# Attention with sketched keys, then a SiLU layer: V arrives as bf16 through GpSimd's queue, and the task list is new

## The chip, the cores and the metric

The kernel runs on one core of a Trainium2 chip. The metric is the device time of one execution in microseconds (us), and lower is better. The core has a matrix engine (TensorE, PE in the profile, with its weight loads as PEld), VectorE (DVE), ScalarE (ACT), GpSimd (POOL) and SyncE (SP), which here only issues transfers. Each engine works through its own instructions in order and waits for the others at semaphores.

## The reference: what is computed

There are four batches and four heads, 1088 tokens and 32 numbers per head. Two small matrices S1 and S2 (8 by 32) make 64 features of each query and key; attention is then linear in these features, and its output goes through a layer of 2048 hidden units.

```python
def phi(x):
    a = np.einsum('rd,bhsd->bhsr', S1, x)
    b = np.einsum('rd,bhsd->bhsr', S2, x)
    return np.einsum('bhsi,bhsj->bhsij', a, b).reshape(*x.shape[:-1], r * r)
q_p, k_p = (phi(q), phi(k))
kv = np.einsum('bhsf,bhsd->bhfd', k_p, v)
z = np.sum(k_p, axis=2)
num = np.einsum('bhsf,bhfd->bhsd', q_p, kv)
den = np.einsum('bhsf,bhf->bhs', q_p, z)[..., None] + 1e-06
# x: (num / den), its heads side by side: 4352 tokens x 128
h = x @ w_in                        # 128 x 2048
g = h * (1.0 / (1.0 + np.exp(-h)))
out = g @ w_out                     # 2048 x 128
```

## The kernel before

Every step of the work is a named task. A batch's function adds tasks under names such as `KV2.3`, and the string `ORDER` lists all names; the tasks are recorded in that order, so each engine gets its instructions in that order too. No scheduler moves anything later. The first number in a name is the batch, or the block of the layer for H, A, O and F.

For each batch b the tasks are these.
- `LK`, `LQ`, `LV` load keys, queries and values. Batch 0's keys and queries come in two parts, and V of every batch in four transfers of 32 partitions each (`load_v`). All of them are issued by SP.
- `KT` transposes keys on DVE, `PK` projects them on PE, `TK` transposes the result back on DVE.
- `KP` forms the 64 products of each key. It is two large DVE instructions for batch 0 and nine small POOL instructions for batches 1 to 3 (`KN`); after each of these POOL also runs a memset of one element, `pause`.
- `VB` casts V from fp32 (`Vx`, two tiles that the batches take in turn) to bf16 (`Vb`). It is on ACT for batches 0 and 1 and on POOL for 2 and 3.
- `KV` sums products times V on PE, `KM` masks the sum, `SE` spreads it over partitions on PE, and `KC` copies it to `KV[b]`.
- `ZS`, `ZT`, `MW`, `WM` make the weights of the denominator in the same way. They go into `WQ[b]`, the weights of the query projection. `WR` copies the fixed part of `WQ` to the other batches, on POOL.
- Queries come in pieces, three for batch 0 and two for each other batch. A piece runs `QT` (transpose, DVE), `PQ` (projection, PE), `TQ` (transpose, DVE), `AW`, `RD`, `RC`, `AQ`, `QP` (denominator and products, DVE), `TN` (transpose, DVE), `NM` (numerators, PE) and `XC` (copy to `xT`, on ACT for batches 0 and 1, on DVE for 2 and 3).

`PK`, `PQ` and `NM` all write the one PSUM tile `pair`, so each of them waits until its reader before has emptied it.

The layer runs over ten blocks of tokens, of 384, seven times 512, 256 and 128. `H` multiplies by two columns of `w_in` (PE), `A` is the SiLU (ACT), `O` multiplies by `w_out` (PE), and `F` moves the block's result out of PSUM (DVE) and stores it through SP. H writes two PSUM tiles by turns (three from block 7 on), so ACT and PE hand buffers to each other. Block 1 needs all pieces of batch 0; block 2 needs the first piece of batch 1; block 4 the first of batch 2, block 5 its second; block 6 the first of batch 3.

`LI` and `LO` load the fp32 weights of the layer; `wi.0` to `wi.3` cast quarters of `w_in` on ACT, and `wo.0` to `wo.3` quarters of `w_out` on POOL. O0.0 and O0.1 need `wo.0`, O0.2 and O0.3 need `wo.1`, and so on. The tasks `f.0` to `f.106` are matmuls of zeros (128 columns) that fill PE's time before the layer starts; each stands at a fixed place of the list.

At the start, the list in the kernel before has on PE: `PQ0.0`, 8 fills, `KV0.0 KV0.5`, 9 fills, `SE0`, 23 fills, `NM0.0`, 10 fills, `PQ0.2`, one fill, `H0.0 H0.1`.

Of the kernel before, what the change touches and what calls it, by code (L numbers as in the profile page):

```python
# [57 lines left out]
H3 = 7  # L58
ORDER = """
S2 LK0.0 LK0.1 begin KT0.0 KT0.1 LQ0.0 QT0.0 LV0.0 LV0.1 LV0.2 LV0.3 begin2 S1 f.0 f.1 f.2 f.3 f.4 f.5 f.6  # L60
f.7 f.8 f.9 SM SN table WQ0 WK L4 f.10 f.11 f.12 f.13 f.14 f.15 f.16 f.17 f.18 f.19 f.20 f.21 f.22 f.23 f.24
PK0.0 PK0.1 TK0.0 TK0.1 f.25 f.26 f.27 f.28 f.29 f.30 f.31 f.32 f.33 ZS0 ZT0 f.34 f.35 f.36 f.37 f.38 f.39
f.40 f.41 MW0 WM0 f.42 f.43 f.44 f.45 f.46 f.47 f.48 f.49 f.50 PQ0.0 KP0.0 KP0.5 TQ0.0 AW0.0 RD0.0 RC0.0
AQ0.0 QP0.0 TN0.0 VB0 f.51 f.52 f.53 f.54 f.55 f.56 f.57 f.58 KV0.0 KV0.5 KM0 f.59 f.60 f.61 f.62 f.63 f.64
f.65 f.66 f.67 SE0 KC0 f.68 f.69 f.70 f.71 f.72 f.73 f.74 f.75 f.76 f.77 f.78 f.79 f.80 f.81 f.82 f.83 f.84
f.85 f.86 f.87 f.88 f.89 f.90 NM0.0 LI.0 wi.0 wi.2 wi.3 XC0.0 wi.1 LQ0.1 LO.0 LO.1 wo.1 wo.0 wo.2 wo.3 WR
LK1 LV1.0 LV1.1 LV1.2 LV1.3 QT0.1 QT0.2 f.91 f.92 f.93 f.94 f.95 f.96 f.97 f.98 f.99 f.100 PQ0.2 TQ0.2 AW0.2
RD0.2 RC0.2 f.101 H0.0 H0.1 A0.0 f.102 PQ0.1 f.103 f.104 f.105 f.106 H0.2 O0.0 A0.1 TQ0.1 AW0.1 AQ0.2 RD0.1
QP0.2 RC0.1 TN0.2 AQ0.1 KT1 QP0.1 LQ1 LK2 LV2.0 LV2.1 LV2.2 LV2.3 LQ2 LK3 H0.3 A0.2 O0.1 H0.4 A0.3 A0.4 O0.2
H0.5 A0.5 NM0.2 O0.3 H0.6 XC0.2 H0.7 A0.6 A0.7 PK1 O0.4 O0.5 O0.6 TK1.1 TK1.0 TN0.1 KP1.0 KP1.1 KP1.2 KP1.3  # L70
KP1.4 KP1.5 KP1.6 KP1.7 KP1.8 ZS1 VB1 ZT1 NM0.1 O0.7 MW1 KV1.0 WM1 QT1.0 LV3.0 LV3.1 LV3.2 LV3.3 LQ3 XC0.1
H1.0 A1.0 H1.1 KV1.1 KV1.2 PQ1.0 KV1.3 KV1.4 H1.2 F0 QT1.1 O1.0 A1.1 KV1.5 H1.3 A1.2 A1.3 TQ1.0 AW1.0 RD1.0
KT2 RC1.0 KV1.6 O1.1 H1.4 O1.2 KV1.7 KV1.8 H1.5 PK2 A1.4 KM1 A1.5 H1.6 SE1 O1.3 O1.4 O1.5 H1.7 AQ1.0 QP1.0
TK2.0 TK2.1 TN1.0 A1.6 KC1 NM1.0 XC1.0 A1.7 O1.6 ZS2 PQ1.1 H2.0 ZT2 A2.0 O1.7 H2.1 KT3 TQ1.1 AW1.1 F1 MW2
PK3 WM2 RD1.1 RC1.1 TK3.1 AQ1.1 QP1.1 TK3.0 TN1.1 QT2.0 QT3.0 A2.1 H2.2 A2.2 KP2.0 KP2.1 KP2.2 KP2.3 KP2.4
KP2.5 VB2 KP2.6 KP2.7 VB3 KP2.8 KP3.0 KP3.1 KP3.2 KP3.3 KP3.4 KP3.5 KP3.6 KP3.7 KP3.8 H2.3 O2.0 A2.3 KV2.0
KV2.1 KV2.2 KV2.3 KV2.4 KV2.5 O2.1 H2.4 O2.2 A2.4 H2.5 O2.3 KV2.6 KV2.7 NM1.1 H2.6 A2.5 H2.7 KV2.8 O2.4
XC1.1 A2.6 ZS3 PQ2.0 ZT3 A2.7 KM2 H3.0 O2.5 O2.6 O2.7 SE2 H3.1 TQ2.0 AW2.0 QT2.1 RD2.0 RC2.0 F2 A3.0 A3.1
H3.2 KC2 PQ2.1 MW3 A3.2 KV3.0 H3.3 A3.3 KV3.1 O3.0 H3.4 KV3.2 O3.1 H3.5 O3.2 A3.4 A3.5 TQ2.1 AQ2.0 QP2.0
TN2.0 H3.6 A3.6 NM2.0 XC2.0 AW2.1 RD2.1 RC2.1 AQ2.1 QP2.1 TN2.1 KV3.3 H3.7 A3.7 O3.3 KV3.4 H4.0 O3.4 KV3.5  # L80
H4.1 O3.5 A4.0 KV3.6 H4.2 A4.1 O3.6 H4.3 O3.7 KV3.7 A4.2 H4.4 A4.3 NM2.1 KV3.8 H4.5 F3 WM3 XC2.1 O4.0 A4.4
A4.5 H4.6 PQ3.0 H4.7 O4.1 A4.6 H5.0 QT3.1 TQ3.0 PQ3.1 AW3.0 TQ3.1 KM3 RD3.0 AW3.1 RC3.0 A4.7 H5.1 A5.0 O4.2
H5.2 O4.3 SE3 KC3 AQ3.0 QP3.0 TN3.0 RD3.1 A5.1 H5.3 A5.2 O4.4 H5.4 O4.5 O4.6 A5.3 H5.5 A5.4 O4.7 H5.6 NM3.0
O5.0 A5.5 H5.7 XC3.0 RC3.1 A5.6 A5.7 O5.1 H6.0 O5.2 O5.3 H6.1 A6.0 O5.4 H6.2 A6.1 A6.2 AQ3.1 QP3.1 TN3.1 F4
NM3.1 O6.0 XC3.1 H6.3 O5.5 A6.3 H6.4 A6.4 O5.6 H7.0 A7.0 H6.5 O6.1 H6.6 O6.2 O6.3 O5.7 A6.5 H6.7 H7.3 A6.6
F5 A6.7 H7.1 A7.1 A7.3 O6.4 O6.5 H7.2 O6.6 O7.0 H7.4 O6.7 H7.6 A7.2 H7.5 O7.1 A7.4 A7.6 H7.7 O7.2 O7.3 O7.4
A7.5 F6 A7.7 H8.0 A8.0 H8.1 O7.5 H8.2 O7.6 A8.1 A8.2 H8.3 A8.3 O7.7 H9.0 O8.0 O8.1 H9.1 O8.2 O8.3 H9.2 A9.0
F7 A9.1 A9.2 O9.0 O9.1 O9.2 F8 F9
# [4 lines left out]
def kernel(  # L93
# [19 lines left out]
    CH = 512  # L113
# [14 lines left out]
    Vx = [sb(f"Vx{i}", [H * NC * D]) for i in range(2)]  # L128
# [422 lines left out]
    for b in range(B):  # L551
        batch(b, KN[b], PIECES[b], XENG[b], KVENG[b])
# [34 lines left out]
```

## Time and profile before

| what | value |
|---|---|
| median of three runs | 94.6 us (94.59, 94.6, 96.18) |
| the profiled execution | 95.22 us, of which the span is 93.4 us |
| granted TensorE clock | 1.0 |
| PE busy | 87.5 us (94%) |
| ACT busy | 76.3 us (82%) |
| DVE busy | 59.3 us (63%) |
| POOL busy | 26.4 us (28%) |
| read from HBM, written | 8.79 MB, 2.23 MB |

The span is the time between the first and last recorded instruction; 1.82 us of the profiled execution lie around it. Times in the profile are counted from the span's start. A waiting matmul that is already in the pipeline counts as busy, so a busy PE is not a PE at its best rate. Issues of transfers are not counted as busy time of the engine that issues them.

### The profile page before, as it was taken

The numbers are of one execution on the slowest core, as the hardware profiler recorded it, in microseconds if no ns is written. First come the engines' busy times: TensorE is split into PE (matmuls) and PEld (weight loads), VectorE is DVE, ScalarE is ACT, GpSimd is POOL, SyncE is SP. The second block draws the span as 40 slices with busy tenths as digits, with TensorE's granted clock in tenths as the row PEclk, the third lists the DMA queues.
The fourth block names the chain that finished last, engine by engine and source line by source line (L and its number), as shares of the span: only waits on it lengthen the run. The fifth ranks groups of instructions, "written<-read, shape, count | busy, mean of one in ns | idle before, by whom it ended". The sixth has DMA issues, their size and how long they took to land.

```text
span 93.4 us, 2184 instructions
## 1 busy us (share of the span) xinstructions
PE 87.5 (94%) x813; PEld 46.7 (50%) x823; DVE 59.3 (63%) x114; ACT 76.3 (82%) x102; POOL 26.4 (28%) x91
## 2 busy tenths in 40 slices
PE   5999989999999999999999999999999999999950
PEld 4948776544543443544444443344344444456940
DVE  2369796999499969983986978489597030300330
ACT  4800687999599868899699999999898999999930
POOL 6700008300993299999900000000000000000000
PEclk9999999999999999999999999999999999999999
DMA  0999999999968730600024003300001404133151
GB/s 19 334 256 343 374 408 318 245 291 238 309 202 222 229 77 14 112 0 7 0 39 73 0 0 63 56 0 0 0 0 29 70 14 85 34 56 60 31 115 50
DMA packets 21898, 11.15 MB, mean 119 GB/s; under 512 B 17152, under 2 KB 20608, under 8 KB 21760
## 3 DMA queue, kind: packets, MB, share of 16 engines
q1 hardware_dynamic: 21704, 10.95, 44.7%
q8 instruction: 6, 0.10, 0.4%
q10 hardware_dynamic: 184, 0.07, 0.3%
q14 instruction: 4, 0.03, 0.1%
HBM read 8.79 MB, written 2.23 MB: 118 GB/s over the span
## 4 chain that ended last, share of the span: by engine, by line
PE 83%; DVE 9%; issue 2%; POOL 2%; DVEq 0%; POOLq 0%
PE hp L181 28%; PE op L181 27%; PE pair L181 14%; PE small L181 14%; DVE QP L192 2%; DVE TQ L435 2%; DVE QU L455 2%; DVE AW L192 1%; DVE TK L368 1%; DVE DN L442 1%; DVE DN L445 1%; DVE AQ L192 0%; POOL hmask L245 0%; POOL Vx L251 0%; DVE OT L540 0%
## 5 line engine op out<-in xcount | busy, mean ns | idle before, releaser
L519 ACT ACTIVATE G<-hp 128x1024 bf16<-128x1024 f32 (+1 forms) x66 | 60.9, 989 | 4.6 <-PE hp L181 2.9
L181 PE MATMUL hp<-xT,w_in_bf 128*128 128x512 bf16 (+3 forms) x137 | 36.2, 355 | 0.2
L181 PE MATMUL op<-G,w_out_bf 128*128 128x512 bf16 (+1 forms) x93 | 25.8, 370 | 0.2
L181 PEld LDWEIGHTS <-w_in_bf 128*128 128x128 bf16 x160 | 13.7, 98 | 13.3 <-issue 2.8
L192 POOL TENSOR_TENSOR KP<-TK 128x256 bf16<-128x256 f32 x27 | 17.0, 631 | 9.2 <-DVE TK L368 9.2
L181 PEld LDWEIGHTS <-w_out_bf 128*128 128x128 bf16 x128 | 11.6, 98 | 12.5 <-issue 1.1
L181 PE MATMUL op<-zeros 128*128 128x128 bf16 x107 | 10.1, 255 | 1.0 <-DVE zeros L240 1.0
L192 DVE TENSOR_TENSOR QP<-AQ,TQ 128x1024 bf16<-128x1024 f32 (+3 forms) x9 | 10.8, 1195 | 0.2
L181 PEld LDWEIGHTS <-zeros 128*128 128x128 bf16 x107 | 7.9, 116 | 3.0 <-issue 1.7
L181 PE MATMUL small<-G,w_out_bf 128*128 128x512 bf16 x31 | 8.8, 379 | 0.1
L435 DVE STREAM_TRANSPOSE TQ<-pair 128x512 f32<-128x512 f32 (+3 forms) x9 | 6.1, 675 | 3.7 <-PE pair L181 2.8
L546 DVE STREAM_TRANSPOSE OT<-small 128x512 f32<-128x512 f32 x2 | 1.4, 716 | 9.3 <-PE small L181 9.3
L355 DVE STREAM_TRANSPOSE KT<-Kx 128x1152 f32<-128x1152 f32 (+1 forms) x5 | 5.6, 1135 | 2.2 <-DMA Kx<-in_k_dram 2.1
L546 DVE STREAM_TRANSPOSE OT<-op 128x512 f32<-128x512 f32 (+1 forms) x6 | 4.0, 667 | 4.1 <-PE op L181 4.1
L181 PEld LDWEIGHTS <-KP 128*128 128x128 bf16 x72 | 4.3, 98 | 4.0 <-issue 0.4
L455 DVE STREAM_TRANSPOSE QU<-QP 128x512 f32<-128x512 f32 (+3 forms) x9 | 6.0, 665 | 0.2
L424 DVE STREAM_TRANSPOSE QT<-Qx 128x512 f32<-128x512 f32 (+3 forms) x9 | 5.7, 653 | 0.3 <-DMA Qx<-in_q_dram 0.3
L181 PE MATMUL pair<-QT,WQ 64*64 64x256 f32 (+3 forms) x72 | 5.7, 389 | 0.1
L181 PE MATMUL small<-Vb,KP 128*128 128x64 bf16 x72 | 5.3, 193 | 0.1
L519 ACT ACTIVATE G<-pair 128x1024 bf16<-128x1024 f32 x5 | 5.2, 1037 | 0.0
L189 POOL CAST w_out_bf<-w_out_f 128x512 bf16<-128x512 f32 x4 | 2.3, 612 | 9.9 <-DMA w_out_f<-in_moe_w_out_dram 9.9
L187 DVE CAST xT<-pair 128x512 bf16<-128x512 f32 (+4 forms) x6 | 3.4, 615 | 2.2 <-PE pair L181 2.2
(68 smaller groups left out, 73.0 us busy)
## 6 DMA issues: line engine op xcount, KB each, us to landing
Vx<-in_v_dram SPq DMA_DIRECT2D x12, 144.0 KB, 9.1
Kx<-in_k_dram SPq DMA_DIRECT2D x3, 544.0 KB, 12.3
Qx<-in_q_dram SPq DMA_DIRECT2D x3, 544.0 KB, 8.8
w_in_f<-in_moe_w_in_dram SPq DMA_DIRECT2D x1, 1024.0 KB
w_out_f<-in_moe_w_out_dram SPq DMA_DIRECT2D x2, 512.0 KB, 9.2
out_dram<-OT SPq DMA_DIRECT2D x16, 64.0 KB, 1.9
Vx<-in_v_dram SPq DMA_DIRECT2D x4, 112.0 KB, 7.2
Qx<-in_q_dram SPq DMA_DIRECT2D x1, 352.0 KB, 7.8
```

What stands on the lines that cost most here:

```text
L181: nc.tensor.matmul(dst, w, x, start=start, stop=stop, tile_position=pos, **kw)
L187: nc.vector.tensor_copy(out=out_, in_=in_)
L189: nc.gpsimd.tensor_copy(out=out_, in_=in_)
L192: (nc.vector if eng == "D" else nc.gpsimd).tensor_tensor(out=out_, in0=a, in1=c, op=ALU.mult)
L355: o.add(f"KT{b}{at}", lambda c0=c0, c1=c1: nc.vector.transpose(out=view(kt[:, :], c0 * 32, (32, c1 - c0), (P, NC), (1, 32)), in_=Kx[b][:, ...
L368: o.add(f"TK{b}.{r}", lambda r=r: nc.vector.transpose(out=view(tk[:, :], 16 * r, (32, NC), (NC * 32, 2), (1, 16)), in_=view(pair[:, :], r ...
L424: o.add(f"QT{b}.{p}", lambda n0=n0, n1=n1: nc.vector.transpose(out=qt[:, n0 * 64: n1 * 64], in_=Qx[b][:, n0 * 64: n1 * 64]))
L435: o.add(f"TQ{b}.{p}", lambda at=at, m=m: nc.vector.transpose(out=tq[:, at * 32: (at + 2 * m) * 32], in_=view(pair[:, :], 0, (CH, 2), (1, m ...
L442: o.add(f"RD{b}.{p}", lambda at=at, rn=rn: nc.vector.tensor_reduce(out=dn[:, at: at + rn], in_=view(aw[:, :], at * 9, (9, rn), (1, 9)), ax ...
L455: o.add(f"TN{b}.{p}", lambda at=at, rn=rn: nc.vector.transpose(out=qu[:, at * 64: (at + rn) * 64].bitcast(FP32), in_=qp[:, at * 64: (at + ...
L519: nc.scalar.activation(out=view(gb[:, :], 0, (stride, per), (1, ntok)), in_=view(hb[:, :], 0, (stride, per), (1, ntok)), func=ACT.Silu)
L546: nc.vector.transpose(out=t[:, :ntok], in_=ob[:, :ntok])
```

## The change

V of every batch is now loaded by GpSimd's queue, straight into the bf16 tiles, so that the transfer itself makes bf16 of fp32. The tiles `Vx` and the four `VB` tasks are gone. The products of batch 3's keys are two DVE instructions (`KP3.0`, `KP3.5`) in place of nine on POOL. `HOLDS` makes the first transfer of V of batch 1 wait for the first half of `w_out`. The list is new. The diff below leaves out functions whose new forms issue the same instructions as before: `project_q`, `tokens_q`, `numerators` and `back` can now also cut a piece of more than 16 units and put parts on other engines, and with the tables given they do neither.

```diff
-KN = [[('D', 0, 5), ('D', 5, 9)], [('P', 0, 1), ... ('P', 8, 9)], [('P', 0, 1), ...], [('P', 0, 1), ...]]
+KN = [[('D', 0, 5), ('D', 5, 9)], [('P', 0, 1), ... ('P', 8, 9)], [('P', 0, 1), ...], [('D', 0, 5), ('D', 5, 9)]]
-VB_ENG = 'AAPP'
-HOLDS = {}
+HOLDS = {'LV1.0': 'LO.0'}
...
-    Vx = [sb(f"Vx{i}", [H * NC * D]) for i in range(2)]
...
     def load_v(b, c):
         n = min(NC, NY - c * NC)
-        return nc.sync.dma_start(
-            view(Vx[b % 2][32 * c: 32 * (c + 1), :], 0, (NC * D, H), (1, n * D)),
+        return nc.gpsimd.dma_start(
+            view(Vb[b][32 * c: 32 * (c + 1), :], 0, (NC * D, H), (1, n * D)),
             AP(tensor=v.tensor, offset=v[b, 0, c * NC].offset,
                ap=[[NY * D, 32], [S * D, H], [1, n * D]]))
...
     def begin2():
-        nc.gpsimd.memset(view(Vx[1][96:P, :], (NY - 3 * NC) * D, (NC * D, H),
-                              (1, (4 * NC - NY) * D)), 0.0)
         nc.gpsimd.memset(view(AW[1][:, :], 8, (9, 2 * NN)), 1e-6)
         for b in range(1, B):
             nc.gpsimd.memset(view(WQ[b][:, :], 16, (32, 2), (1, 16)), 0.0)
             nc.gpsimd.memset(view(Kx[b][:, :], NY * D, (1, (4 * NC - NY) * D)), 0.0)
+            nc.gpsimd.memset(view(Vb[b][96:P, :], (NY - 3 * NC) * D, (NC * D, H),
+                                  (1, (4 * NC - NY) * D)), 0.0)
...
-    for b in range(B):
-        o.add(f"VB{b}", lambda b=b: copy(VB_ENG[b], Vb[b], Vx[b % 2]))
```

The new list, cut to the stretches that the prediction speaks of:

```
S2 LK0.0 LK0.1 begin KT0.0 S1 table f.0 ... f.9 SM WK SN L4 KT0.1 WQ0 LV0.0
begin2 LV0.1 LV0.2 LV0.3 LQ0.0 LI.0 LQ0.1 LO.0 LO.1 LK1 LQ1 LK2 LQ2 LK3 LQ3 wo.0 LV1.0 LV1.1 LV1.2 LV1.3
wo.2 wo.1 WR LV2.0 wo.3 QT0.0 f.10 ... f.24
PK0.0 PK0.1 TK0.0 TK0.1 KP0.5 KP0.0 f.25 ... f.33 ZS0 ZT0 f.34 ... f.41 MW0 WM0 f.42 ... f.50
PQ0.0 TQ0.0 AW0.0 RD0.0 RC0.0 AQ0.0 QP0.0.0 TN0.0.0 f.51 ... f.72
KV0.0 wi.2 wi.1 KV0.5 KM0 wi.0 f.73 ... f.81 SE0 KC0 f.82 ... f.90 NM0.0 XC0.0.0 wi.3 QT0.2 QT0.1 f.91 ...
f.100 PQ0.2 TQ0.2 AW0.2 RD0.2 RC0.2 f.101 H0.0 H0.1 A0.0 f.102 PQ0.1 A0.1 f.103 ... f.106
H0.2 A0.2 O0.0 O0.1 H0.3 O0.2 H0.4 A0.3 TQ0.1 AQ0.2 AW0.1 KT1 RD0.1 QP0.2.0 RC0.1 A0.4 PK1 H0.5 A0.5 TK1.1
AQ0.1 TN0.2.0 TK1.0 KP1.0 ... KP1.8 QP0.1.0 TN0.1.0 O0.3 H0.6 O0.4
H0.7 A0.6 ZS1 NM0.2 O0.5 O0.6 A0.7 XC0.2.0 ZT1 NM0.1 MW1 KV1.0 KV1.1 O0.7 XC0.1.0 H1.1 A1.1 KT2 PK2 QT1.0
...
O1.6 O1.7 XC1.0.0 H2.0 A2.0 LV2.1 LV2.2 LV2.3 LV3.0 LV3.1
KP2.0 KP2.1 KP2.2 LV3.2 LV3.3 KP2.3 ... KP2.8 H2.1
...
PQ2.0 A2.4 H2.6 KV2.2 KV2.3 KV2.4 KV2.5 O2.3 TQ2.0 KP3.0 QT2.1 AW2.0 RD2.0 RC2.0 AQ2.0 QP2.0.0 TN2.0.0 A2.5
...
O3.2 A3.7 QT3.1 XC2.0.0 WM3 H4.0 A4.0 PQ3.0 KP3.5 AQ2.1 QP2.1.0 TQ3.0 TN2.1.0 H4.1 A4.1 KV3.0 H4.2 O3.3 O3.4
...
H5.5 NM3.0 A5.4 A5.5 H5.6 O4.7 O5.0 A5.6 H5.7 XC3.0.0
TN3.1.0 NM3.1 XC3.1.0 F4 H6.0 O5.1
```

## The prediction

> **What bounds the kernel now.** I read the busy shares first, then the chain that ended last, in order of time, then the timelines of ACT and POOL and the landing times of V. Busy times and shares:
>
> ```profile
> PE 87.5 (94%) x813; PEld 46.7 (50%) x823; DVE 59.3 (63%) x114; ACT 76.3 (82%) x102; POOL 26.4 (28%) x91
> PE 83%; DVE 9%; issue 2%; POOL 2%; DVEq 0%; POOLq 0%
> ```
>
> PE bounds most of the span, and POOL, where the change works, carries 2% of the chain. The 9% of DVE lie early, as the chain in order of time shows (start, length, what):
>
> ```profile
> 13.43 0.59 DVE QU L455
> 14.02 0.04 issue
> 14.06 0.36 PE pair L181 x7
> ...
> 19.36 0.42 DVE QU L455
> 19.78 0.04 issue
> 19.82 0.34 PE pair L181 x8
> ...
> 23.08 0.47 DVE QU L455
> 23.55 0.04 issue
> 23.59 0.36 PE pair L181 x7
> ```
>
> The reader sees each piece of batch 0 end with its transpose on DVE (`TN0`), for which PE's numerators wait: at 14.02, 19.78 and 23.55. Block 1 starts at 24.6. From there on PE hardly stops. A pair of 512-column matmuls takes 0.432 in the chain; blocks 1 to 9 are 124 of them, 53.6 us, and what is left of attention is about 10.3 (PK 2 x 0.65, PQ 3.75, NM 2.3, KV 1.6, ZS, MW and SE 1.4). That is 63.9 of the 65.5 us up to the last matmul at 90.1. So after 24.6 only 1.6 us can be won, and between 15.5 and 24.6 about 1 us, if no DVE link of the early chain becomes shorter.
>
> **The early chain, DVE part.** The new list leaves the order of DVE's work up to `TN0.0` as it was, with the same durations, and the same number of fills ahead of `PQ0.0`. So `TN0.0` ends at 14.0 again, and that is the earliest time of `NM0.0`. Nothing is won here.
>
> **VB0 goes from ACT, and V comes otherwise.** This is what ACT did before (start, length, what):
>
> ```profile
> 9.74 1.16 ACT L185 ACTIVATE Vb<-Vx 128x1152 bf16<-128x1152 f32 x1
> 11.73 0.52 ACT L279 ACTIVATE KM<-small,pmask 128x64 bf16<-128x64 f32 x2 [0.83 <-PE small L181]
> 12.61 0.38 ACT L185 ACTIVATE KV<-small 128x256 bf16<-128x256 f32 x1 [0.36 <-PE small L181]
> ```
>
> V was used from 10.95 on, and KV0 was ready at 12.99, one us before `NM0.0` could use it. The new list spends this us: 22 fills (0.061 each in this stretch: 0.67 for 10, in the chain) stand ahead of `KV0.0` instead of 8, so its turn comes at 10.55 + 1.38 = 11.93; sums 0.55, mask 0.55 with its wait, then `wi.0` 0.62 stands ahead of `KC0` 0.38: 14.03. The cast's 1.16 on ACT is therefore worth nothing, and each tenth that V is later than 12.0 is a tenth later for everything, because DVE's chain for the other two pieces starts from `XC0.0`.
>
> When does V land? The trace has no transfer issued by POOL. The first comes behind the memsets of `begin`, at 3.1; the rest behind `begin2`, which takes 1.4 now and about 2.1 with two more memsets (0.31 each). For the issue itself the bounds are SP's issue row (0.31 at least, 0.43 in this stretch) and a whole cast of V on POOL (1.19 undisturbed). I take 0.63, the row of POOL's small product, as a POOL instruction over 128 partitions. Then the last issue ends at 3.1 + 2.1 + 4 x 0.63 = 7.7. From issue to landing:
>
> ```profile
> Vx<-in_v_dram SPq DMA_DIRECT2D x3, 144.0 KB, 3.9
> ...
> Vx<-in_v_dram SPq DMA_DIRECT2D x3, 144.0 KB, 10.1
> ```
>
> The first row holds the issues before 6 us, the second those between 6 and 14: V of batch 1, far back in a full queue. A queue of its own does not stand behind SP's, but the 16 DMA engines are shared and fully busy from 3 to 25 us in both lists. I take the longest of the first three, 4.4: V lands at 12.1, loss 0.15 to 0.2. Bounds: 3.8 after issues of 0.31 gives 10.3, no loss; issues of 1.19 and 4.4 give 14.4, loss 2.3; a landing of 8.6, the median of all V transfers, gives 16.3, loss 4.3.
>
> The Trainium skill, page "DMA: Bandwidth & Descriptors", section "Anatomy of one DMA — SWDGE (gpsimd) path", gives a transfer of this queue as 2.0 us plus bytes by 436 GB/s. That is 2.3 us for 144 KB; by it alone, V would land at 10.0 and the loss would be nothing. The rows above already show 3.8 to 4.4 in this kernel's traffic.
>
> **SP without V.** SP issues 16 transfers less (0.31 to 0.55 each). `LI` moves from 4.43 to about 2.5. `w_in` was cast at 12.89, behind `KC0` and not behind its transfer, so only the earlier casts `wi.2` and `wi.1` use that; their slots on ACT were idle. Keys and queries of batches 1 to 3 land earlier, and nobody waited for them. Bytes from HBM stay the same. Worth: 0, hidden by the DVE chain.
>
> **POOL's queue.** New behind `wo.0`, which waits for the first half of `w_out`, are four issues of V of batch 1, then `wo.2`, `wo.1`, `WR`, one issue, `wo.3` and `KP1`. The hold on `LV1.0` adds nothing, for `wo.0` waits for the same landing. Before:
>
> ```profile
> 14.09 1.17 POOL L189 CAST w_out_bf<-w_out_f 128x512 bf16<-128x512 f32 x2 [9.53 <-DMA w_out_f<-in_moe_w_out_dram]
> 15.64 1.17 POOL L189 CAST w_out_bf<-w_out_f 128x512 bf16<-128x512 f32 x2 [0.39 <-DMA w_out_f<-in_moe_w_out_dram]
> ```
>
> With the same landing, `wo.1` ends at 14.09 + 0.6 + 4 x 0.63 + 1.17 = 18.4. Its user `O0.2` has its turn at 18.34 (H0.0 at 15.5, and from there pairs of 384 columns of 0.32 and 0.5 for `PQ0.1`), so it is just in time. At 1.19 for an issue it is 2.2 late. About half of that is covered, since H1 waits for DVE until 24.5 anyway and PE then has only 3.9 us of work to place: loss 1.0. V of batch 1 is issued up to 17.2; `KV1.0`, now ahead of the first H of block 1, has its turn at 24. With 4.4 it lands at 21.6; with 10.1 at 27.3.
>
> **KP3 to DVE, VB2 and VB3 gone, the new order.** DVE gets the two instructions that batch 0 has, 1.49 + 1.22 = 2.7 us. POOL loses nine products (0.63 each) and two casts, which had slowed DVE while they ran: one cast took 2.23 instead of 1.19 beside a QP of 1.67 instead of 1.36. So some 0.5 comes back. Following the new list pair by pair from 24.5 with these rows, `TN2.0` ends at about 46.8 (50.3 before), with `KP3.0` in it; `XC2.0` ends at 51.3, with PE waiting 0.4 for it; `TN3.1` ends near 67.1, just when `NM3.1`, now ahead of `H6.0`, has its turn. DVE is busy 37.0 of the 45.4 us from 24.6 to 70, so 8.4 idle us must take 2.7 more of work and an end that is 2.8 earlier: 2.9 are left over. If that cover is gone, PE stalls at `NM3.1` for what DVE is late. Counting PE's finished work at the same places, the new list is ahead by 0.36 at H3.0 (43.8 before), 0.2 at H4.0 and 0.3 to 0.4 at H6.0 (67.9). The tail after that is the same. Gain taken: 0.3. Its bounds are -1.0 (DVE late) and the 2.6 of idle time above.
>
> **Sum.** 95.22 - 0.3 + 0.2 = 95.1 for the profiled execution, whose own time lies 0.6 above the median of the three runs. On the median, 94.6 - 0.1 = **94.5**.
>
> **Rivals.**
> 1. *V lands too late* (slower). One mechanism in two places: at `KV0.0` once V comes after 12.0, at `KV1.0` after 24. For it: the DMA share is 0.9 to 1.2 in every us from 3 to 25, latency grew to 10.1 there, and one us of cover was given away. Against: the first V transfers took 3.8 to 4.4. Price 2.2 to 4.3: 96.7 to 98.9. Chance 0.21.
> 2. *Issuing waits for VectorE* (slower). For it, a cast on POOL doubled beside a two-input DVE product. If writing a transfer's list waits in the same way, the last issues of V of batch 0 wait for `KP0`, which ends at 10.22: 10.2 + 0.6 + 4.4 = 15.2, a loss of 3.1, 97.6. Against: POOL's issues read no tile, and KT, QT and TK have one input. Chance 0.04. The Trainium skill, page "SBUF — State Buffer", section "SBUF: two separate sides", says that VectorE can lock GpSimd out while it writes such lists, but only in instructions that use both ports; the doubled cast agrees with its lock between two-input instructions and GpSimd instructions that read, and no row here shows an issue.
> 3. *POOL's issues are long*, 1.19, but V still lands in time: the stall at `O0.2`, 95.5. Chance 0.13.
> 4. *The gaps close* (faster): the new order takes 1.2 to 2.3 of the 2.6 us of idle PE time, 92.3 to 93.4. For it: DVE is 3.5 us ahead at `TN2.0`, and PE gets `PK1` to do before 20 us. Against: the DVE chain to 24.5 stays. Chance 0.12.
>
> That V comes by another way than stated is no open case: the old tiles and casts are gone from the program.
>
> **How the numbers follow.** The forecast, 93.5 to 95.6, has 0.50. The range leaves out the lower half of rival 4 and the upper half of rivals 1 and 2 (under 0.2 together): 93.0 to 97.4. About 2%, 1.9 us, is what a measurement of this kernel tells from no change: the limits are 92.7 and 96.5. Faster: half of rival 4 and 0.01 more, 0.07. Slower: rivals 1 and 2 and 0.01 of a late DVE, 0.26. Within 2%: 0.67.
>
> **What would show it.** Right: V's landing or the turn of `KV0.0` near 12, `NM0.0` at 14 to 14.3, block 1 at 24.5, POOL's second `w_out` casts done by 18.4, no wait of PE at `KV1.0` and `NM3.1`, last matmul near 90. Rival 1 shows as PE waiting for a transfer at the sums of V, rival 2 as issues on POOL that end with DVE's products, rival 3 as PE waiting for POOL near 18, rival 4 as block 1 before 24. I am wrong altogether if a start earlier than 15.5 shows for H0.0, since I see nothing that could shorten it.

## The result, and the profile after

The changed kernel takes 99.0 us (median of four runs, 98.29 to 99.5) against 95.39 us for the kernel before in the same session (94.59 to 96.87). The ratio is 1.042, with a 95% interval of 1.033 to 1.051: the change makes the kernel **slower**, and 99.0 lies above the forecast range. In all ratios below, executions that were disturbed are left out, so that a ratio is not always the quotient of the two medians.

The profiled execution of the changed kernel took 98.29 us, with a span of 96.5 us (before: 95.22 and 93.4). Busy times and the chain by engine:

```profile
PE 88.8 (92%) x823; PEld 46.7 (48%) x823; DVE 60.4 (63%) x116; ACT 74.9 (78%) x100; POOL 27.4 (28%) x89
PE 72%; DMA 9%; POOL 6%; ACT 4%; issue 2%; SPq 1%; DVE 1%; ACTq 0%; POOLq 0%
```

The chain has new members. DVE's 9% have become 1%, and DMA and POOL together have 15%. The chain in order of time names them (start, length, what):

```profile
3.11 0.67 POOL Vb L209
...
6.06 1.02 POOL Vb L209 x2
7.08 7.24 DMA Vb<-in_v_dram
14.32 0.14 issue
14.45 0.70 PE small L173 x18
15.24 0.53 ACT KM L279 x2
15.81 0.27 PE small L173 x2
16.08 0.50 PE op L173 x9
16.60 0.36 PE pair L173 x8
```

The last part of V of batch 0 was issued by 7.62, as forecast (7.7), and took until 14.32 to land. The forecast was 12.1. The sums `KV0` run at 14.45 instead of 10.95, `NM0.0` at 16.60 instead of 14.06, and `H0.0` at 18.06 instead of 15.52. PE's timeline has `KV0` and `H0.0` before (the second cut by the window's end), then `H0.0` in the changed kernel:

```profile
10.95 0.68 PE L181 MATMUL small<-Vb,KP 128*128 128x64 bf16 x18
...
15.52 0.65 PE L181 MATMUL hp<-xT,w_in_bf 128*128 128x384 bf16 x3
```

```profile
18.06 0.81 PE L173 MATMUL hp<-xT,w_in_bf 128*128 128x384 bf16 x4
```

These are the landing times (name, queue, count, KB as written, median us from issue to landing) of the issues up to 9.7 us:

```profile
Vb<-in_v_dram POOLq DMA_DIRECT2D x3, 72.0 KB, 6.9
Qx<-in_q_dram SPq DMA_DIRECT2D x1, 192.0 KB, 5.4
Vb<-in_v_dram POOLq DMA_DIRECT2D x1, 56.0 KB, 7.2
```

V in SP's queue had needed 3.8 to 4.4. The second row is the first part of the queries: they came at 7.49 instead of 5.74. DVE's and PE's timelines show what followed:

```profile
7.49 0.58 DVE L425 STREAM_TRANSPOSE QT<-Qx 128x384 f32<-128x384 f32 x1 [1.88 <-DMA Qx<-in_q_dram]
```

```profile
6.66 0.68 PE L173 MATMUL op<-zeros 128*128 128x128 bf16 x9
8.85 0.38 PE L173 MATMUL small<-TK 128*32 128x32 f32 x18 [1.52 <-DVE TK L366]
...
11.00 0.92 PE L173 MATMUL pair<-QT,WQ 64*64 64x192 f32 x8
11.86 2.07 PE L173 MATMUL op<-zeros 128*128 128x128 bf16 x22
14.45 0.69 PE L173 MATMUL small<-Vb,KP 128*128 128x64 bf16 x18 [0.53 <-DMA Vb<-in_v_dram]
```

`TK0` stands behind `QT0.0` on DVE, so PE was without work for 1.52 us. Then its clock fell: `PQ0.0` took 0.92 instead of 0.56, and 22 fills took 2.07, where 1.40 is usual. So `KV0`'s turn was at 13.9 in this execution, and V was 0.5 later still. In this execution either delay alone would have made most of the loss; the experiments below tell which one always comes.

POOL's timeline shows the issues and the casts of w_out:

```profile
3.05 0.73 POOL L209 DMA_DIRECT2D Vb<-in_v_dram  x1
...
6.01 1.61 POOL L209 DMA_DIRECT2D Vb<-in_v_dram  x3
14.56 0.69 POOL L189 CAST w_out_bf<-w_out_f 128x512 bf16<-128x512 f32 x1 [6.93 <-DMA w_out_f<-in_moe_w_out_dram]
15.20 2.14 POOL L209 DMA_DIRECT2D Vb<-in_v_dram  x4
17.34 1.17 POOL L189 CAST w_out_bf<-w_out_f 128x512 bf16<-128x512 f32 x2
```

An issue takes 0.54 (the first 0.73), against 0.63 forecast, and `wo.1` ends at 18.5, against 18.4.

Where the 3.1 us of span went: +2.54 up to `H0.0`. From `H0.0` to the first H of block 1, -0.60 (8.49 instead of 9.09). From there to the start of the last copy of DVE, +0.33 (65.85 instead of 65.52). Behind that copy, +0.8, in the last stores; this piece is between 3.0 and 3.9 us in all profiles, also of kernels whose ends are the same. So 0.8 of the 3.1 may be nothing but this variation. The ratio stands for 4.0 us; where the other 0.9 lies no trace shows.

### The profile page after: what moved, and what is told of

Its sections match the earlier page's. It is cut to its first block, busy times and chain, and to the rows that moved or that the text cites. A ratio compares the mean times of both kernels' runs of the same rounds, so it can differ in the third digit from the quotient of the medians.

```text
span 96.5 us, 2168 instructions
## 1 busy us (share of the span) xinstructions
PE 88.8 (92%) x823; PEld 46.7 (48%) x823; DVE 60.4 (63%) x116; ACT 74.9 (78%) x100; POOL 27.4 (28%) x89
## 3 DMA queue, kind: packets, MB, share of 16 engines
q0 software_dynamic: 2304, 1.12, 9.3%
## 4 chain that ended last, share of the span: by engine, by line
PE 72%; DMA 9%; POOL 6%; ACT 4%; issue 2%; SPq 1%; DVE 1%; ACTq 0%; POOLq 0%
PE hp L173 28%; PE op L173 22%; PE small L173 12%; PE pair L173 11%; DMA Vb<-in_v_dram 7%; ACT G L542 3%; DMA out_dram<-OT 2%; POOL Vb L209 2%; SPq L515 1%; POOL Vb L268 1%; DVE OT L569 1%; ACT KM L279 1%; POOL SEL L262 0%; POOL hmask L245 0%; POOL Vb L251 0%
## 5 line engine op out<-in xcount | busy, mean ns | idle before, releaser
L542 ACT ACTIVATE G<-hp 128x1024 bf16<-128x1024 f32 (+1 forms) x66 | 61.6, 989 | 5.7 <-PE hp L173 4.7
L173 PE MATMUL hp<-xT,w_in_bf 128*128 128x512 bf16 (+3 forms) x142 | 37.5, 356 | 0.1
L173 PE MATMUL op<-G,w_out_bf 128*128 128x512 bf16 (+1 forms) x96 | 26.3, 371 | 0.0
L192 POOL TENSOR_TENSOR KP<-TK 128x256 bf16<-128x256 f32 x18 | 11.8, 656 | 4.1 <-DVE TK L366 4.0
L209 POOL DMA_DIRECT2D Vb<-in_v_dram x16 | 8.9, 560 | 0.0
L173 PEld LDWEIGHTS <-KP 128*128 128x128 bf16 x72 | 3.7, 98 | 3.3 <-DVE AQ L192 0.7
L192 DVE TENSOR_TENSOR KP<-TK 128x1024 bf16<-128x1024 f32 (+1 forms) x4 | 5.3, 1340 | 0.0
```

The lines of the kernel that those rows point to most:

```text
L173: nc.tensor.matmul(dst, w, x, start=start, stop=stop, tile_position=pos, **kw)
L192: (nc.vector if eng == "D" else nc.gpsimd).tensor_tensor(out=out_, in0=a, in1=c, op=ALU.mult)
L209: return nc.gpsimd.dma_start(view(Vb[b][32 * c: 32 * (c + 1), :], 0, (NC * D, H), (1, n * D)), AP(tensor=v.tensor, offset=v[b, 0, c * NC]. ...
L542: nc.scalar.activation(out=view(gb[:, :], 0, (stride, per), (1, ntok)), in_=view(hb[:, :], 0, (stride, per), (1, ntok)), func=ACT.Silu)
```

## The experiments

All twelve kernels compute the whole reference. The starts (us) come from the timelines of PE and DVE; "waits" names what the turn waited for.

| kernel | KV0 | H0.0 | block 1 | last copy | time, ratio to before (95%) |
|---|---|---|---|---|---|
| before | 10.95 | 15.52 | 24.61 | 90.13 | 95.39 |
| changed | 14.45 | 18.06 | 26.55 | 92.40 | 99.0, 1.042 (1.033 to 1.051) |
| 1 V0 by SP | 11.24 | 15.88 | 25.95 | 91.82 | 98.2, 1.029 (1.017 to 1.040) |
| 2 V by POOL, old list | 13.67 | 18.89 | 27.63 | 93.71 | 100.1, 1.056 (1.042 to 1.070) |
| 3 the same in fp32 | 15.83 | 21.93 | 30.67 | 96.19 | 102.1, one run |
| 4 w_in held | 11.79 | 19.57 | 29.81 | 95.68 | 101.6, one run |
| 5 KP3 on POOL | 14.30 | 17.91 | 27.85 | 93.86 | 99.7, 1.042 (1.025 to 1.059) |
| 6 w_in in quarters | 14.75 | 19.46 | 27.88 | 93.73 | 98.5, 1.031 (1.016 to 1.046) |
| 7 V0, V1 by SP | 11.56 | 15.59 | 26.54 | 92.40 | 97.7, 1.022 (1.005 to 1.039) |
| 8 V0 issued first | 12.76 | 16.93 | 25.59 | 91.46 | 97.3, 1.021 (1.013 to 1.029) |
| 9 V0 first, V1 early | 13.44 | 17.46 | 26.47 | 92.35 | 97.9, 1.024 (1.016 to 1.033) |
| 10 as 7, K1 sooner | 12.00 | 16.02 | 25.30 | 91.16 | 96.9, 1.014 (1.009 to 1.020) |
| 11 V0 by SP, V1 early | 11.35 | 15.23 | 25.06 | 90.93 | 95.7, 1.006 (1.002 to 1.009) |
| 12 as 11, V1 behind w_in | 11.44 | 15.24 | 25.40 | 91.25 | 96.5, 1.019 (1.014 to 1.024) |

(V0 and V1 are V of batches 0 and 1, K1 the keys of batch 1; "block 1" is its first H.)

**1. V of batch 0 by SP's queue, the rest as changed.**

```diff
-        return nc.gpsimd.dma_start(
-            view(Vb[b][32 * c: 32 * (c + 1), :], ...
+        eng, dst = (nc.sync, Vx0) if b == 0 else (nc.gpsimd, Vb[b])
+        return eng.dma_start(
+            view(dst[32 * c: 32 * (c + 1), :], ...
...
-KT0.1 WQ0 LV0.0 begin2 LV0.1 LV0.2 LV0.3 LQ0.0 LI.0
+KT0.1 WQ0 begin2 LQ0.0 LV0.0 LV0.1 LV0.2 LV0.3 LI.0
...
-KV0.0 wi.2 wi.1 KV0.5 KM0
+VB0 KV0.0 wi.2 wi.1 KV0.5 KM0
```

> Changed kernel, but V of batch 0 comes as before: fp32 through SP's queue, right behind the first queries, and cast by ACT (1.16 us) ahead of the sums. Batches 1 to 3 stay on GpSimd's queue, list and KP3 stay new. Theory 'start' (all of the loss comes before H0.0, because V and the first queries of batch 0 land late): first queries land at 5.7 and not 7.5, H0.0 starts at 15.5 to 15.8 and not 18.2, and since the new list is 0.4 quicker after that, the time is 0.2 to 0.6 us under the kernel before. Theory 'list' (the new order or KP3 on VectorE costs time too): H0.0 at 15.5, but the time stays 1 us or more above the kernel before.

`KV0` runs at its turn, `H0.0` is back at 15.88, and yet the time is only 0.8 below the changed kernel's median and 2.8 above the kernel before. By the words of the expectation that is the second theory, but what the trace shows is not the order or KP3 as such. (The profiled execution, 96.97, is 1.2 shorter than the other three of this kernel, so it shows less of the loss than they have.) The second place of the loss appears, first in the chain, then on PE:

```profile
14.93 1.77 POOL Vb L211 x3
16.70 8.67 DMA Vb<-in_v_dram
```

```profile
25.51 0.28 PE L174 MATMUL small<-Vb,KP 128*128 128x64 bf16 x4 [0.70 <-DMA Vb<-in_v_dram]
```

V of batch 1 lands at 25.4, and `KV1.0` stands ahead of the first H of block 1. In the changed kernel itself the late `H0.0` had hidden this. Smaller delays: PE waited 0.84 for `KT1`, and on ACT the mask `KM0` stood behind `wi.2` and `wi.1`, which waited for w_in until 12.02.

**2. The kernel before, with V by POOL's queue as bf16 and so without the casts; 3. the same in fp32, with the old tiles and casts.**

```diff
-        return nc.sync.dma_start(
-            view(Vx[b % 2][32 * c: 32 * (c + 1), :], ...
+        return nc.gpsimd.dma_start(
+            view(Vb[b][32 * c: 32 * (c + 1), :], ...
```

> Kernel before with one part of the change alone: V of all batches as bf16 through GpSimd's queue, no casts; old list, KP3 on GpSimd. V of batch 0 is issued in one go from 3.1 to 5.2 us, ahead of begin2. Theory 'start': V of batch 0 lands at 12.5 to 14.5, 2 to 3 us after its turn at 10.95, the first queries land late as well because w_in now stands right behind them, and the time is 1.5 to 3 us above the kernel before. Theory 'list': the time stays within 0.7 us of the kernel before.

> Kernel before with V through GpSimd's queue, but fp32 into the old tiles, casts kept where they were. It differs from the run above in the conversion alone. If the conversion makes the transfer slow, V of batch 0 lands near 7 (issue at 3.1 to 5.2 plus the 3.8 to 4.4 that SP's queue took) and H0.0 starts at 15.5 to 16. If it is the queue beside SP's traffic, V lands at 12 to 14 here too and H0.0 starts at 17 to 19, with the cast of 1.2 us behind it.

V by the queue, without the rest of the change, costs 5.6%, more than the whole change; the forecast of 1.5 to 3 us was too low. The four transfers were issued from 3.07 to 5.42 in one go, and still landed at 13.5:

```profile
Vb<-in_v_dram POOLq DMA_DIRECT2D x3, 72.0 KB, 8.2
Vb<-in_v_dram POOLq DMA_DIRECT2D x1, 56.0 KB, 8.7
```

`H0.0` comes 3.37 later, more than V alone explains: 23 fills stand behind `SE0` in the old list, and part of it, about 0.9, is a slow clock (`KV0` took 1.12 instead of 0.68, the nine fills behind it 1.15 instead of 0.67). In fp32 V lands at 14.6, not earlier, so leaving out the conversion doesn't bring V back to 7. What the conversion itself costs is not separated by this: in fp32 the transfer writes twice the bytes, in 192 packets instead of 576.

**4. w_in, and all that SP issues behind it, held until V of batch 0 has landed.**

```diff
-HOLDS = {'LV1.0': 'LO.0'}
+HOLDS = {'LV1.0': 'LO.0', 'LI.0': 'LV0.3'}
```

> Changed kernel with one more hold: w_in, and all that stands behind it on SP, is issued only when V of batch 0 has landed. If SP's traffic is what slows GpSimd's transfers, V of batch 0, whose last issue ends at 7.6, lands within 2 to 3 us of it, near 10, and the first queries land at 5.7. If GpSimd's queue is slow by itself, V lands at 13 or later as without the hold. The time itself gets no better: w_in then lands 3 us or more after V, and its casts stand ahead of the mask on ACT, so H0.0 is expected at 17 to 19 either way.

```profile
Vb<-in_v_dram POOLq DMA_DIRECT2D x3, 72.0 KB, 2.5
...
Vb<-in_v_dram POOLq DMA_DIRECT2D x1, 56.0 KB, 2.4
```

The same issues now land in 2.4 to 2.7 us, and `KV0` runs at 11.79, its turn. The time is worse, since w_in lands at 14.5 and the mask stands behind its casts. SP's traffic beside V is therefore the cause of the late landing, not POOL's issue and not the queue as such. The Trainium skill, page "DMA: Bandwidth & Descriptors", section "Anatomy of one DMA — SWDGE (gpsimd) path", gives 2.3 us for such a transfer by its formula; the trace agrees in this kernel and where the DMA engines idle (2.3 to 2.5 for the issues after 28 us of the changed kernel), and not beside SP's queue (6.1 to 8.8 there).

**5. The products of batch 3 back on POOL, as nine small instructions; all else as changed.**

```diff
-KN = [..., [('D', 0, 5), ('D', 5, 9)]]
+KN = [..., [('P', 0, 1), ('P', 1, 2), ... ('P', 8, 9)]]
```

> The key products of batch 3 go back to POOL as nine small instructions, all else as in the changed kernel. If the move of these products to DVE cost nothing, as I read the equal lengths from block 1 to the last copy (65.7 us after, 65.5 before), the start stays as it is (H0.0 near 18.1, block 1 near 26.7) and the time stays within 0.5 us of the changed kernel's, 98.5 to 99.5. If the two large DVE products are part of the loss, block 4 and the last copy come earlier and it is 0.5 to 2 us faster.

From block 1 to the last copy this kernel takes 66.01, the changed one 65.85, so the move to DVE costs nothing that these two profiles show. The run tells more about the start. The queries landed at 6.9, the clock did not fall, and `KV0`'s turn was at 12.5; it was V alone that set the time:

```profile
11.12 1.40 PE L173 MATMUL op<-zeros 128*128 128x128 bf16 x22
14.30 0.68 PE L173 MATMUL small<-Vb,KP 128*128 128x64 bf16 x18 [1.78 <-DMA Vb<-in_v_dram]
```

`H0.0` is at 17.91, within 0.15 of the changed kernel. So the late queries and the slow clock seen there are not needed for the loss; V's landing at 14.3 is enough. The changed kernel's own executions agree: a stretch of 3.41 us at half the clock takes 0.017 off the mean granted clock, and two of the four had 0.990 and 0.994, too much to hold one. They took 99.09 and 98.92, the other two 98.29 (0.976) and 99.50 (0.974). Behind that, V of batch 1 took 10.6 us this time and `KV1.0` waited 1.36: both places of the loss in one profile.

**6. w_in in four column quarters, 2 KB rows instead of 8 KB.**

```diff
-LQ0.0 LI.0 LQ0.1
+LQ0.0 LI.2 LI.1 LI.0 LI.3 LQ0.1
...
-    for i in range(WIN):
-        ... load(f"LI.{i}", ... w_in_f[r0:r1, :], moe_w_in[r0:r1, :])
+    for i in range(4):
+        load(f"LI.{i}", ... w_in_f[:, i * quarter: (i + 1) * quarter], ...)
```

> The changed kernel with the transfer of w_in cut into four column quarters: the same bytes, but rows of 2 KB in place of 8 KB. Theory turns: the DMA engines serve the two queues packet by packet, so V's short rows (1152 bytes read) lose most beside 8 KB rows. Then V of batch 0 lands near 11 to 12.5 instead of 14.3, the first queries still wait behind part of w_in, H0.0 starts near 16.5 to 17.3, and the time is 97.0 to 98.2. Theory bytes: the engines share bandwidth by bytes and V waits for the bytes ahead of it, whatever the rows' size. Then V lands at 14 to 14.5 and the time is that of the changed kernel, 98.3 to 99.5.

The queries came sooner (6.14), but `KV0` started at 14.75: by its landing, the theory of turns fails here. (The time decides little: the profiled execution, 99.32, is the slowest of four, and of the others 97.63 lies in the first forecast, 98.30 and 98.72 in the second. The profile names `QT` on DVE as what `KV0` waited for, but `KV0` doesn't read it; V's last part landed at 14.6.) Counting packets shows why. V's first transfer began earlier (5.3 us instead of 7.3), but the other three, issued from 6.0 on, had no packet before 10.0. From there on other rows than those of w_in stand beside them, in both kernels (about 1.1 KB a packet between 11 and 13 us). Two parts of a mechanism are visible in other profiles. In some stretches where both queues have work, they take turns, one packet each, though the packets differ in size. These are queue, packets, MB and share of the 16 engines' time, first for 7 to 9 us of kernel 8 (SP's rows are those of w_in), then for 12 to 13 us of kernel 11:

```profile
q1 hardware_dynamic: 82, 0.59, 80.3%
q0 software_dynamic: 83, 0.05, 16.1%
```

```profile
q1 hardware_dynamic: 145, 0.17, 60.1%
q0 software_dynamic: 145, 0.07, 55.3%
```

A batch of V is 576 packets of about 0.5 KB (as written), so beside 7 KB packets it gets a twelfth of the bytes in such a stretch. This is not the whole reason. Other stretches show no such turns: 97 packets of POOL's queue to 434 of SP's from 9 to 11 us in the changed kernel, 192 to 590 from 7 to 14 us in kernel 3. And there V's 192 large packets needed as long (7.3 to 13.8 us) as its 576 small ones in kernel 2 (7.2 to 13.2). The Trainium skill, page "DMA: Bandwidth & Descriptors", section "Queues, rings and completion order", says that an engine takes the queues in turn, a packet at a time; these two rows agree, if the page's packet is what the profile counts as one, which no run shows. The other part: with SP's queue full, the first packet of V mostly comes 4 us or more after the issue (changed kernel: issue at 3.05, first packet at 7.3; kernel 2: 3.07 and 7.2; kernel 5: 3.06 and 7.7; kernel 11: 5.36 and 9.7; kernel 12: 12.31 and 16.3), but after 1.5 us in kernel 4, 1.9 in kernel 8 and 2.3 in this one. What happens in these 4 us no run shows, so why V takes 7 us beside SP's traffic stays open.

**7. The new list with V of batches 0 and 1 by SP's queue as fp32; V of batches 2 and 3 on POOL's queue; mask and `KC0` ahead of the casts of w_in.**

```diff
+        eng, dst = (nc.sync, Vx[b]) if b < 2 else (nc.gpsimd, Vb[b])
...
-LO.0 LO.1 LK1 LQ1 ... wo.0 LV1.0 LV1.1 LV1.2 LV1.3 wo.2 wo.1 WR LV2.0 wo.3
+LO.0 LO.1 LK1 LV1.0 LV1.1 LV1.2 LV1.3 LQ1 ... wo.0 wo.1 wo.2 wo.3 WR VB1
...
-KV0.0 wi.2 wi.1 KV0.5 KM0 wi.0 ... SE0 KC0 ... XC0.0.0 wi.3
+VB0 KV0.0 KV0.5 KM0 ... SE0 KC0 wi.0 wi.1 ... XC0.0.0 wi.2 wi.3
```

> The new list with V of batches 0 and 1 by SP's queue as fp32 and cast (batch 0 on ACT, batch 1 on POOL after w_out's casts); V of batches 2 and 3 stays on GpSimd's queue as bf16, issued at 30 to 36 us when the DMA engines idle; the mask and KC0 stand ahead of the casts of w_in on ACT. If V's lateness in its two places, and the mask behind these casts in the first experiment, are the whole loss, then KV0.0 and KV1.0 wait for no transfer, H0.0 starts near 15.5, block 1 near 24.5, and the time is from 0.6 us under to 0.3 over the kernel before. If the new list or the products of batch 3 on DVE cost something of their own, block 1 or the last copy is later by it and the time is 1 us or more above the kernel before.

`H0.0` is at 15.59 and no PE instruction waits for V, but block 1 is at 26.54, 10.95 after `H0.0`. The new list is late in another way, on DVE:

```profile
19.55 1.38 DVE L358 STREAM_TRANSPOSE KT<-Kx 128x1152 f32<-128x1152 f32 x1 [1.01 <-DMA Kx<-in_k_dram]
```

The list has `KT1` ahead of `QP0.2`; in the kernel before it stood behind, and started at 19.83. With `H0.0` on time, the keys of batch 1 become the last to come.

**8. V of batch 0 issued first of all by POOL.**

```diff
-S2 LK0.0 LK0.1 begin ... WQ0 LV0.0 begin2 LV0.1 LV0.2 LV0.3 LQ0.0
+S2 LV0.0 LV0.1 LV0.2 LV0.3 LK0.0 LK0.1 begin ... WQ0 begin2 LQ0.0
```

> The changed kernel with one edit: GpSimd issues the four transfers of V of batch 0 first of all (about 0.4 to 2.8 us), ahead of the memsets of begin; nothing else moves. Theory backlog: V is slow because it is issued when the rows of w_in, which SP issues at 2.5 us, stand ahead of it at the DMA engines. Then V lands before 9, KV0.0 starts at its turn near 12, and H0.0 near 16.1 (0.6 for the later memsets and masks). Theory queue: GpSimd's queue gets little while SP's queue holds anything, whenever V is issued. Then V lands at 13 to 14.5 again and H0.0 starts near 18. In both, V of batch 1 is still issued at 15 to 17 and lands 8.5 to 10.5 us later, so block 1 starts at 25.9 to 27.4 and the time is 97.5 to 98.7 by the first, 98.5 to 99.7 by the second.

`KV0` waits for nothing (12.76, its turn). V landed at about 12.0, between the two forecasts (before 9; 13 to 14.5), but in time. The queue was not quicker for being first: the four transfers landed 4.1 to 9.0 us after their issues, the last one in the longest time. They were only issued early enough. What is left of the delay of `H0.0`, 1.4, comes from the memsets and masks of `begin`, which the issues push back by 2.9 us (`TK0` at 8.30 instead of 6.71). The time, 97.3, is 0.2 under what the theory of the backlog gave.

**9. As 8, with V of batch 1 issued behind `begin2`, mask and `KC0` ahead of the casts of w_in, `LK1` ahead of `LO.1`.** Against kernel 8:

```diff
-HOLDS = {'LV1.0': 'LO.0'}
+HOLDS = {}
-begin2 LQ0.0 LI.0 LQ0.1 LO.0 LO.1 LK1 ... wo.0 LV1.0 LV1.1 LV1.2 LV1.3 wo.2 wo.1
+begin2 LV1.0 LV1.1 LV1.2 LV1.3 LQ0.0 LI.0 LQ0.1 LO.0 LK1 LO.1 ... wo.0 wo.1 wo.2
...
-KV0.0 wi.2 wi.1 KV0.5 KM0 wi.0 ... SE0 KC0 ... XC0.0.0 wi.3
+KV0.0 KV0.5 KM0 ... SE0 KC0 wi.0 wi.1 ... XC0.0.0 wi.2 wi.3
```

> As the kernel with V of batch 0 issued first, and three edits more: V of batch 1 is issued behind begin2 (4.5 to 7 us), without the hold on w_out; the mask and KC0 stand ahead of the casts of w_in on ACT; keys of batch 1 are issued ahead of the second half of w_out. If transfers that come too late are all that is wrong with the changed kernel, then KV0.0, KT1 and KV1.0 wait for nothing, H0.0 starts near 16.1, block 1 near 24.6 (8.4 to 8.5 us later), and with 65.9 us from there to the last copy the time is 95.2 to 96.2. If the new list has a cost of its own, block 1 comes after 25.5 without a wait of PE or DVE for a transfer.

Neither V is waited for, yet the time is not better than in 8, and my forecast missed by 1.7 us. `H0.0` is 0.5 later than in 8: eight fills behind `ZS0` took 1.03 instead of 0.62, and `XC0.0` stood behind two casts of w_in. Then it is 9.0 to block 1. The early V takes turns with w_out, which is cast 1.4 later than in 8, and beside the casts DVE is slower (`AQ0.2` 0.69 instead of 0.20), so `KT1` starts at 20.28, although its keys are there. Of the 1.9 that block 1 is later than forecast (26.47 for 24.6), 1.4 lie before `H0.0` (17.46 for 16.1). By the words of the expectation the rest, 0.5, is a cost of the list itself; that it comes from more DVE work ahead of `QP0.2` is argued, not shown.

**10. As 7, with the keys of batch 1 ahead of the second half of w_out.**

```diff
-LO.0 LO.1 LK1
+LO.0 LK1 LO.1
```

> The kernel with V of batches 0 and 1 by SP's queue, and one edit: keys of batch 1 are issued ahead of the second half of w_out, so that they land 1 to 2 us sooner. There the transpose KT1 waited until 19.5 for them, and it stands ahead of the products of the second piece of batch 0 on DVE. If that is why block 1 started 10.9 us after H0.0 there and 8.5 in the changed kernel, it starts 8.5 to 9.1 after H0.0 now, at 24.2 to 24.8, and the time is 1.7 to 2.3 us below that kernel's, at the kernel before's. If the casts of V on POOL beside VectorE are the cause, block 1 stays after 25.5.

`KT1` runs at 18.24 without a wait, and block 1 starts 9.28 after `H0.0` instead of 10.95, a little over the forecast of 8.5 to 9.1. The time is only 0.8 below kernel 7's, where 1.7 to 2.3 was forecast. Most of what is left to 8.5 is one DVE product beside POOL's cast of V and its first small product, on DVE's and POOL's timelines:

```profile
21.84 1.82 DVE L193 TENSOR_TENSOR QP<-AQ,TQ 128x768 bf16<-128x768 f32 x1
```

```profile
21.71 1.15 POOL L190 CAST Vb<-Vx 128x1152 bf16<-128x1152 f32 x1 [0.20 <-issue]
22.82 1.32 POOL L193 TENSOR_TENSOR KP<-TK 128x256 bf16<-128x256 f32 x1
```

The same product takes 0.92 in the changed kernel. So the keys' place in the queue explains most of kernel 7's delay after `H0.0`; the cast and the product on POOL fit what is left, which no run tested alone.

**11. V of batch 0 by SP, V of batch 1 by POOL's queue as bf16 but issued at 5.4 to 7.7; `LK1` ahead of `LO.1`; only `wi.0` ahead of `XC0.0`. 12. As 11, with V of batch 1 held until w_in has landed.** The edits of 11 against kernel 1, then those of 12 against 11:

```diff
-HOLDS = {'LV1.0': 'LO.0'}
+HOLDS = {}
-begin2 LQ0.0 LV0.0 LV0.1 LV0.2 LV0.3 LI.0 LQ0.1 LO.0 LO.1 LK1 ... wo.0 LV1.0 LV1.1 LV1.2 LV1.3 wo.2 wo.1 WR LV2.0 wo.3
+begin2 LV1.0 LV1.1 LV1.2 LV1.3 LQ0.0 LV0.0 LV0.1 LV0.2 LV0.3 LI.0 LQ0.1 LO.0 LK1 LO.1 ... wo.0 wo.1 wo.2 WR wo.3
-VB0 KV0.0 wi.2 wi.1 KV0.5 KM0 wi.0 ... SE0 KC0 ... XC0.0.0 wi.3 ... A0.0
+VB0 KV0.0 KV0.5 KM0 ... SE0 KC0 wi.0 ... XC0.0.0 wi.1 wi.2 ... A0.0 wi.3
...
-H2.0 A2.0 LV2.1
+H2.0 A2.0 LV2.0 LV2.1
```

```diff
-HOLDS = {}
+HOLDS = {'LV1.0': 'LI.0'}
-begin2 LV1.0 LV1.1 LV1.2 LV1.3 LQ0.0 ... LQ3 wo.0
+begin2 LQ0.0 ... LQ3 LV1.0 LV1.1 LV1.2 LV1.3 wo.0
```

> The new list with V of batch 0 by SP's queue (fp32, cast on ACT), V of batch 1 on GpSimd's queue as bf16 but issued behind begin2 (about 5 to 8 us), keys of batch 1 ahead of the second half of w_out, and only wi.0 ahead of XC0.0 on ACT. No cast of V on POOL is left to slow VectorE, which cost QP0.1 0.9 us in the kernel with V of both batches by SP. If late transfers and these side effects are the whole difference between the two lists, then nothing waits for a transfer after 8 us, H0.0 starts at 15.5 to 16.0, block 1 8.4 to 8.6 us later (24.0 to 24.6), the last copy ends near 90.3, and the time is within 0.5 us of the kernel before's (ratio 0.995 to 1.006). If the new list has a cost of its own beyond transfers, block 1 comes after 25.2 and the ratio stays at 1.014 or above.

> As the kernel with V of batch 0 by SP's queue and V of batch 1 early on GpSimd's, and one edit: V of batch 1 waits until w_in has landed (it is then issued at about 12.5 to 14.7 us instead of 5.4 to 7.7), so that it no longer takes its share of the transfers before w_out's first half. There the first casts of w_out came at 17.1, H0.3 waited 1.1 us for O0.0, and the casts slowed products on DVE beside them. If that is what is left of the new list's loss, w_out lands near 15, H0.3 follows H0.2 in 0.7 us, V of batch 1 lands by 23, block 1 starts at 24.0 to 24.5 and the ratio to the kernel before is 0.992 to 1.000. If the issue at 13 to 15 makes V of batch 1 land after 24.3, or the casts slow DVE wherever they stand, block 1 stays at 25 and the ratio at 1.004 to 1.010.

Kernel 11 is the best version found: `H0.0` 0.29 earlier than before the change, and the time 0.6% above it (interval 0.2 to 0.9%). By block 1, at 25.06, it lies between the two forecasts (24.0 to 24.6, and 25.2). The early V of batch 1 takes turns with w_out, whose first half is cast at 17.1 instead of 14.1; `O0.0` waited for it on PE:

```profile
17.89 0.82 PE L174 MATMUL op<-G,w_out_bf 128*128 128x384 bf16 x4 [0.65 <-POOL w_out_bf L190]
```

`KT1` waited 0.27 for its keys as well. Kernel 12 removes the wait for w_out (w_out is cast at 14.97, `NM0.1` at 23.09), and then one wait is left, on PE, behind a transfer of 10.7 us from its issue:

```profile
24.96 0.28 PE L174 MATMUL small<-Vb,KP 128*128 128x64 bf16 x4 [1.28 <-DMA Vb<-in_v_dram]
```

Both forecast ratios were missed (1.019 came), but V did land after 24.3, as the second theory had it. Of the 1.9%, 1.3 us are this wait. So in these two kernels V of batch 1 on POOL's queue either takes from w_out or comes late itself. No version is faster than the kernel before.

## Why the prediction was wrong

**The step that failed** is the landing of V: "A queue of its own does not stand behind SP's ... I take the longest of the first three, 4.4". The issue went as forecast (0.54 for 0.63, the last ending at 7.62 for 7.7); the landing took 6.7 from there, so V came at 14.3 for 12.1. The rows I took, 3.8 to 4.4, were of transfers that stood ahead of w_in in SP's queue. In the new kernel V comes behind w_in's issue. Rows nearer to that place stood in the same trace, 8.6 over all V transfers and 10.1 for those far back in the queue, and I used them for the bounds alone. Kernels 1, 2, 4 and 5 show that this term by itself makes the delay of `H0.0`: with V by SP it is gone (15.88), with V alone by POOL it is there, without SP's traffic V lands 2.4 to 2.7 after its issue, and with the queries and the clock better `H0.0` is still at 17.91. Why the landing takes 7 us beside SP's traffic stays open.

**The mechanism was right, and it was rival 1**, to which I gave 0.21. It has the two places named there: `KV0.0` (in the changed kernel, and in 2, 3, 5 and 6) and `KV1.0` (in 1, 5 and 12, and slightly in 8). Its price was put at 2.2 to 4.3 us; 4.2% of 95.4 is 4.0, in that range partly by luck: the profiles show 3.1, with 0.8 of it in the last stores. "Each tenth that V is later than 12.0 is a tenth later for everything" held up to `H0.0` (V 2.3 later than 12.0, `H0.0` 2.54 later than before); at block 1 1.94 were left.

**The early chain.** "`TN0.0` ends at 14.0 again" was wrong by 1.4: the first queries landed at 7.49. "SP without V ... Worth: 0" had not seen that what stood behind the first queries would change from V to w_in. By kernel 5 it was not needed for the loss, and with the same order on SP the queries came anywhere between 5.5 (kernel 2) and 7.5, so its cause stays open. (22 fills at 0.061 are 1.34, where the sum for `KV0`'s turn has 1.38; nothing hangs on it.)

**POOL's queue.** Forecast and measured: `wo.1` 18.4 and 18.5, last issue of V of batch 1 17.2 and 17.34, its landing 21.6 to 27.3 and 25.4 (kernel 1), 27.3 (kernel 5). Rival 3 (long issues) falls with 0.54.

**Rival 2**, issues that wait for VectorE, falls in kernel 9, where four issues from 8.27 to 10.44 ran beside the large products of DVE (9.19 to 11.82) and took 0.54 each.

**KP3 and the new order.** `TN2.0` ends 22.4 after block 1 starts (22.3 forecast), `TN3.1` 42.7 (42.6), PE waits nowhere, and the part from block 1 to the last copy is 65.85 to 65.88 in ten kernels with the new list and its products of batch 3 on DVE, whatever happened before it: that is the work of PE, as read from the profile before. The gain of 0.3 was forecast for the part after block 1, and there the profile shows a loss of 0.33: this term had the wrong sign. With the 0.60 won before block 1 it makes 0.27, close to 0.3 by luck. And the 0.60 was there only because `H0.0` was late; with `H0.0` on time (1, 7, 10, 11, 12) the new list needs 9.3 to 11 us to block 1, for its earlier users of K1, V and w_out then wait for their transfers (in 10 they do not, and a product is slow beside a cast). That the list is tighter on transfers I had weighed for V alone. Rival 4 did not come.

## What to carry to other kernels

Price a transfer by a row with the same traffic ahead of it and beside it, not by the same transfer's row at another place: here V of a batch took 2.4, 4.4 or 7 to 8 us a transfer. In these kernels a second queue was no way past a full one: V of batch 0 landed later on it than on the first, and what V of batch 1 won by an early issue, w_out lost. Where fills or casts cover a landing by one us only, moving that landing can be the whole change, whatever it saves on the engines.

## What the runs showed of the hardware that I had not expected

- With SP's queue full, POOL's queue mostly moved no packet for 4.0 to 4.7 us after its first issue (the five kernels named above; 1.9 in kernel 8, 2.3 in kernel 6). Then, in some stretches, it moved one packet for each of SP's, though of another size (83 to 82, 145 to 145), in others far fewer (97 to 434, 192 to 590). On this queue V as fp32 landed no earlier than as bf16 (14.6 against 13.5, one run).
- A product on DVE beside a cast and then a product on POOL took twice its time in kernel 10 (1.82 for 0.92), and a small one beside casts over three times its own in kernel 9 (0.69 for 0.20).
- TensorE's granted clock halves some time after PE has been without work, for 3.4 us or twice that. These are windows of the changed kernel (from and to, us, busy time and number of PE's matmuls, clock, DMA share, GB/s):

```profile
8.00:9.00 1.00, 0.15 (x17) 1.00 0.95 287
9.00:10.00 1.00, 1.00 (x31) 0.94 1.05 306
10.00:11.00 1.00, 1.00 (x9) 0.50 1.11 351
11.00:12.00 1.00, 1.00 (x11) 0.50 1.20 269
12.00:13.00 1.00, 1.00 (x11) 0.50 1.24 265
13.00:14.00 1.00, 0.93 (x13) 0.85 1.16 353
```

A mean of 0.94 is 0.12 us at half the clock, 0.85 is 0.30: the low stretch lasts 0.12 + 3 + 0.30 = 3.42 us. In the same way kernels 2 and 6 give 3.42, kernel 4 gives 3.40, and kernel 3 gives 6.84. The Trainium skill, page "TensorE: Matmul & The Clock Gate", section "Part 1: The HAM clock gate (the "warmup" mystery)", says that the clock is set by a monitor in free-running windows of 3.4 us, and the trace agrees in this length. The page has the low clock after an idle window; here 1.5 us without work were enough in the changed kernel, and 1.8 us in kernel 5 were not. What decides it these runs do not show.
